# Twelve gate and value pairs by Strassen instead of eleven, in a fused attention and two-layer MoE kernel on one core

## The chip, the cores and the metric

One Trainium2 chip, one of its cores. The time is the device time of one execution in microseconds (us). TensorE (PE) multiplies matrices, VectorE (DVE) and ScalarE (ACT) work element by element, GpSimd (POOL) does a little of the same, and SyncE (SP) issues nearly all DMAs. Each engine takes its own instructions strictly in the order in which the program lists them and waits at the head of its list until the semaphores of that instruction are set.

## The reference, cut to what matters

```python
attn = softmax(causal(q @ k.T / 8)) @ v            # 2 x 12 heads, 448 tokens, 64 wide
x = attn as [896 tokens, 768]
h = x @ w_in;  g = h * clip(h + 3, 0, 6) / 6       # d_ff 2048
y = g @ w_out                                      # [896, 768]
rms = sqrt(mean(y * y, axis=-1) + 1e-6)
yn = y / rms * rms_g
out = (silu(yn @ w_gate) * (yn @ w_val)) @ w_out2  # d_ff 1536
```

The change touches the step from `y` to the products with `w_gate` and `w_val`.

## The kernel before, in words

Tokens lie on the free axis: the 896 tokens are two groups, 0 and 1, of NT = 448. The 768 features are six blocks of 128 partitions, the 1536 hidden features of the second MLP twelve blocks, each with a gate and a value block: a pair m.

Every product of two fp32 numbers is made of three matmuls in fp32r (`mm3`): each operand is split into a high half (a cast on ACT) and a low half (the difference to it, on DVE), and high x high, low x high and high x low are summed in PSUM. A matmul is always 128x128 weights by 128x448 data.

A pair is a product of 2x2 blocks: gate and value weights over two halves of the features (KH = 3 blocks each), times the activations of group 0 and group 1 over the same halves. Done plainly it takes 8 block products of 9 matmuls, 72 in all. By Strassen (the Winograd form) it takes 7, that is 63, with sums of weights (`pair_first`, `pair_second`) and sums of activations. The products are numbered 1 to 7: 1 and 2 need activations of group 0 alone; 7 needs group 0 minus group 1; 6, 5, 4 and 3 need further sums of both. In the names, `yhi7_0` and `ylo7_0` are the halves of block 0 of the activations of product 7, `pthi2_7` and `ptlo2_7` the halves of pair 2's weights for product 7, `phi0_1` and `plo0_1` pair 0's value weights (products 4 and 3), `phi0_0` its gate weights (products 1 and 2).

The program is written in steps. In one step the generator `products()` emits 9 matmuls (AFTER), and `at(d, fn)` lets `fn` emit its ACT, DVE or SP instructions d steps later. So the delays set where an instruction stands in its engine's list; the semaphores set when it runs.

Before the change the first MLP's output product for group 1, `ff1_out(1)`, ends; `ff1_y` evicts each of its six blocks from PSUM and squares it. A matmul with ones (`rms_sum`, named n1) adds the squares over the partitions, `rms_root` takes the root (ACT) and the reciprocal (DVE), and `y_scale` multiplies the six blocks of group 1 by it. Only then can products with group 1 run. In the meantime PE has work with group 0: pair 0 is done plainly (PLAIN = 1, `ff2_plain`), its four block products with group 0 first, then products 1 and 2 of pairs 1 and 2, and then pair 0's four block products with group 1, which need scaled blocks but no sums. After these come the products 7, 6, 5, 4, 3 of pairs 1 and 2, then pair after pair. `y_sums`, `y_more` and `y_last` make the sums, `y_split` and `y_low` their halves.

Weights come as 768 KB loads into four `raw` buffers, are narrowed on ACT (two instructions), joined on DVE (`pair_early_join`) and, for Strassen, summed and split. Pairs 1 and 2 are loaded early, in steps 12, 14, 18 and 20 of `ff1_out(1)` (EARLY); the plain pair comes through the ordinary weight stream (`w_load`, `w_split`, `w_join`).

Of the kernel before, what the change touches and what calls it, by code (L numbers as in the profile page):

```python
# [13 lines left out]
AF = mybir.ActivationFunctionType  # L14
# [7 lines left out]
NK = DM // 128  # L22
# [3 lines left out]
NF2 = FF2 // 128  # L26
NT = B * HS
NP1 = 16
# [1 line left out]
ORDER = (1, 5, 6, 7, 3, 4, 2)  # L30
NSLOT = 75
PREPS = (2, 3.6, 8), (1, 3, 4)
EARLY = (12, 14), (18, 20)
PLAIN = 1
LATE = 10
MASK = -8e9
NRAW, NC_BUF, NW = 4, 3, 5
# [14 lines left out]
def fused_kernel(ctx: ExitStack, tc, qa, qb, ka, kb, v, w_in, w_out, w_gate, w_val, w_out2, rms_g, out):  # L52
# [5 lines left out]
    nc = tc.nc  # L58
# [50 lines left out]
    srcs, kept, parts = [], {}, {}  # L109
    for a in (w_in, w_out):  # L110
        srcs += [a[n] for n in range(NP1)]
    for name in ("in", "out"):
        srcs += [(name, n) for n in range(NP1)]
    for m in range(PLAIN):
        srcs += [w_gate[m], w_val[m]]
    IN2 = 4 * NP1
    OUT2 = IN2 + 2 * PLAIN
    srcs += [(p, n) for p in ORDER for n in range(NN)]
    raws, plain, splits = {}, {}, {}

# [76 lines left out]
    used = set()  # L197

    def w_tile(n, j):

        if n not in used and not IN2 <= n < OUT2:
            used.add(n)
            splits.pop(n - 2, None)
            at(1, w_split)
        return tuple(t[:, j * 128:(j + 1) * 128] for t in splits[n])

    def mm3(ps, w, x, first, last, again=False):

# [239 lines left out]
    def ff1_out(g, w0):  # L448


        for m in range(NK):
            ps = psum(f"y{g}_{m}")[:, :NT]
            for k in range(NF1):
                i = m * NF1 + k
                yield from mm3(ps, w_tile(w0 + i // 6, i % 6), gs[g, k], k == 0, k == NF1 - 1)
            soon(ff1_y, g, m, ps)
        for k in range(NF1):
            gs.pop((g, k))

# [149 lines left out]
    def rms_root(g, ps):  # L609
        nc.scalar.activation(ri[g], ps, AF.Sqrt, bias=eps, scale=1.0 / DM)  # L610
        nc.vector.reciprocal(ri[g], ri[g])
        for k in range(NK):
            at(1 + (k // 2 if g else 2 * k), y_scale, g, k)
        if g:
            for j in range(KH):
                at((5, 6, 6)[j], y_sums, j)

    KH = NK // 2
    ops = {}

    def y_scale(g, k):
        y = ys[g, k]
        nc.vector.tensor_mul(y, y, ri[g])
        at(1, y_split, {(0, 0): 1, (0, 1): 2, (1, 0): 0, (1, 1): 4}[g, k // KH], k % KH, y)

    def y_split(q, j, src):
        hi = slot([128, NT], f"yhi{q}_{j}", F32R)
# [2 lines left out]
        ops[q, j] = (hi, lo)  # L630
        at(1, y_low, q, j, hi, lo, src)

    done = set()

    def y_low(q, j, hi, lo, src):
        nc.vector.tensor_sub(lo, src, f32(hi))
        done.add((q, j))

    def y_sums(j):

        assert (0, j) in done and (4, j) in done
        a21, a22 = ys[1, j], ys[1, j + KH]
        nc.vector.tensor_add(a22, a21, a22)
        nc.vector.tensor_sub(a21, ys[0, j], a21)
        at(1, y_split, 5, j, ys[1, j + KH])
        at(1, y_split, 7, j, ys.pop((1, j)))
        at(1, y_more, j)

    def y_more(j):
        a11 = ys.pop((0, j))  # L650
        nc.vector.tensor_sub(a11, ys.pop((1, j + KH)), a11)
        at(1, y_split, 6, j, a11)
        at((4, 5, 5)[j], y_last, j, a11)

    def y_last(j, s2):
        a12 = ys.pop((0, j + KH))
        nc.vector.tensor_sub(a12, a12, s2)
        at(1, y_split, 3, j, a12)


    ss, spare = {}, []

    def ff2_plain(w0):

        a, b = PLAIN, PLAIN + 1
        splits.pop(w0 - 2, None)
        splits.pop(w0 - 1)
        at(1, pair_third, b)
        at(1, pair_high, b, 0)
        at(2, pair_low, b, 0)  # L670
        for i in range(2):
            at(6 + i, pair_load, b + 1, i)
        at(9, pair_high, a, 1)
        at(13, pair_low, a, 1)
        at(11, pair_high, b, 1)
        at(14, pair_low, b, 1)
        for g in range(2):
            for i in range(2):
                ps = psum(f"f{g}_{i}")[:, :NT]
                for k in range(NK):  # L680
                    q = ((1, 2), (0, 4))[g][k // KH]
                    yield from mm3(ps, w_tile(w0 + i, k), ops[q, k % KH], k == 0, k == NK - 1)
                if i == 0:
                    at(1 if g else 3, ff2_gate, g, 0, ps)
                else:
                    at(2, ff2_val, g, 0, ps)
                if g == 0:
                    spare.append(ps)
                else:
                    splits.pop(w0 + i)  # L690
            if g == 0:
                yield from ff2_products((q, m) for q in (1, 2) for m in (a, b))
        for j in range(KH):
            ops.pop((0, j))

    def ff2_gate(g, m, ps):
        t = slot([128, NT], f"t{g}_{m}")
        nc.scalar.activation(t, ps, AF.Silu)
        ss[g, m] = t

    def ff2_val(g, m, ps):
        t = ss.pop((g, m))
        nc.vector.tensor_mul(t, ps, t)
        left_ready(g, m, t)


    praw, pc, ph = {}, {}, {}
# [7 lines left out]
    def pair_early(m, loads):  # L715

        for i in range(2):
            at(loads[i], pair_load, m, i)
            at(loads[i] + 5, pair_early_narrow, m, i)
        at(loads[1] + 7, pair_first, m)  # L720
        at(loads[1] + 8, pair_second, m)

    def pair_early_narrow(m, i):
        raw = praw.pop((m, i))
        narrowed(f32(raw[:, :, 1]), raw, False)
        at(1, pair_early_join, m, i, raw)

    def pair_early_join(m, i, raw):
        pc[m, i] = []
# [94 lines left out]
    fb, fh = {}, {}  # L824

    def ff2_strassen():
        a, b = PLAIN, PLAIN + 1
        order = [(7, a), (7, b), (6, a), (6, b), (5, a), (4, a), (5, b), (3, a), (4, b)]
        for m in range(b + 1, NF2):
            order += [(1, m), (3, m - 1)] + [(q, m) for q in (7, 6, 2, 5, 4)]  # L830
        order.append((3, NF2 - 1))
        yield from ff2_products(order)
        spare.clear()

    def ff2_products(order):
        b = PLAIN + 1
        for q, m in order:
            if (q, m) == (7, b) or q == 1 and b < m < NF2 - 1:
                pair_begin(m + 1)
            if q == 1 and m + 1 == NF2:  # L840
                state["limit"] = len(srcs)
                for n in range(NC_BUF):
                    at(1 + n, w_load)
                for n in range(NW - 1):
                    at(4 + n + 3 * (n // 3), w_split)
                for p in range(NF2 // 2):
                    at(1 + p // 2, a_fetch, ORDER[0], p)
                    at(4 + p // 2, a_split, ORDER[0], p)
                for p in range(3):
                    at(5 + p, a_fetch, ORDER[1], p)  # L850
            name = {1: "x", 2: "x", 7: "r", 4: "r"}.get(q, "y")
            if q in (1, 7):
                fb[name, m] = psum(f"f{name}_{m}")[:, :NT]
            ps = fb[name, m]
            for j in range(KH):
                yield from mm3(ps, pair_tile(q, m, j), ops[q, j], q in (1, 7) and j == 0, j == KH - 1,
                               q not in (1, 7))
                if m == NF2 - 1:
                    ops.pop((q, j))
            soon(ff2_combine, q, m)  # L860
# [58 lines left out]
    def products():  # L919
        yield from ff1_in(0, 0)  # L920
        yield from ff1_out(0, NP1)
        plan_preps(0, *PREPS[0])
        yield from ff1_in(1, 2 * NP1)
        plan_preps(PREPS[0][2], *PREPS[1])
        for m, loads in enumerate(EARLY, PLAIN):
            pair_early(m, loads)
        at(EARLY[0][1] + 9, pair_third, PLAIN)
        at(30, pair_high, PLAIN, 0)
        at(31, pair_low, PLAIN, 0)
        yield from ff1_out(1, 3 * NP1)  # L930
        yield from ff2_plain(IN2)
        yield from ff2_strassen()
        yield from strassen(OUT2)

# [116 lines left out]
```

## Time and profile before

| | |
|---|---|
| median of 3 runs | 572.06 us (571.95 to 573.84) |
| profiled execution | 571.2 us |
| its span | 569.4 us |
| PE busy | 559.0 us (98%), 3039 matmuls |
| DVE busy | 411.9 us (72%) |
| ACT busy | 391.7 us (69%) |
| granted TensorE clock, mean | 0.997 of full speed |

Busy shares are averages over the span; matmuls overlap, so PE at 98% does not say that it ran without waits. The chain of waits names what ended last at each step; the timeline gives start, duration and the idle time before an instruction, with the engine that ended it. Times in the timeline count from the start of the span.

### The profile page before, as it was taken

The numbers are of one execution on the slowest core, as the hardware profiler recorded it, in microseconds if no ns is written. First come the engines' busy times: TensorE is split into PE (matmuls) and PEld (weight loads), VectorE is DVE, ScalarE is ACT, GpSimd is POOL, SyncE is SP. The second block draws the span as 40 slices with busy tenths as digits, with TensorE's granted clock in tenths as the row PEclk, the third lists the DMA queues.
The fourth block names the chain that finished last, engine by engine and source line by source line (L and its number), as shares of the span: only waits on it lengthen the run. The fifth ranks groups of instructions, "written<-read, shape, count | busy, mean of one in ns | idle before, by whom it ended". The sixth has DMA issues, their size and how long they took to land.

```text
span 569.4 us, 9052 instructions
## 1 busy us (share of the span) xinstructions
PE 559.0 (98%) x3039; PEld 488.9 (86%) x3039; DVE 411.9 (72%) x809; ACT 391.7 (69%) x774; POOL 83.8 (15%) x130
## 2 busy tenths in 40 slices
PE   8799999999999999999999999999999999999997
PEld 6457777777899999999999998899999999999996
DVE  4776676867654645999666769988987976966861
ACT  7997878888876855887574858665767664754430
POOL 4665626262200100000000100000000000000000
PEclk9989999999999999999999999999999999999999
DMA  8958676765587964799899803063745607685841
GB/s 225 293 167 265 221 247 207 247 209 199 190 295 264 328 225 169 229 316 386 302 349 398 290 0 129 0 253 135 282 147 189 223 34 261 195 274 194 279 142 64
DMA packets 51231, 125.59 MB, mean 221 GB/s; under 512 B 6768, under 2 KB 30256, under 8 KB 51184
## 3 DMA queue, kind: packets, MB, share of 16 engines
q1 hardware_dynamic: 50752, 124.66, 64.5%
q8 instruction: 24, 0.39, 0.3%
q10 hardware_dynamic: 432, 0.34, 0.2%
q14 instruction: 23, 0.19, 0.1%
HBM read 93.36 MB, written 31.62 MB: 220 GB/s over the span
## 4 chain that ended last, share of the span: by engine, by line
PE 89%; ACT 6%; DVE 3%; issue 1%; ACTq 0%; DVEq 0%
PE y L211 8%; PE y L215 8%; PE y L213 8%; PE h L215 7%; PE h L211 7%; PE h L213 7%; ACT sm L338 4%; PE f L211 4%; PE f L213 4%; PE f L215 4%; PE o L398 3%; PE t L372 3%; PE s L321 3%; PE fr L213 2%; PE fr L215 2%; PE fr L211 2%
## 5 line engine op out<-in xcount | busy, mean ns | idle before, releaser
L193 DVE TENSOR_TENSOR wlo<-c,whi 128x768 fp32r<-128x768 f32 x87 | 85.1, 983 | 20.1 <-ACT whi L187 19.1
L187 ACT CAST whi<-c 128x768 fp32r<-128x768 f32 x87 | 72.3, 837 | 34.1 <-DVE c L171 16.0
L215 PE MATMUL h<-xh,wlo 128*128 128x448 f32 x192 | 71.4, 372 | 0.0
L213 PE MATMUL h<-xl,whi 128*128 128x448 f32 x192 | 70.8, 369 | 0.0
L211 PE MATMUL y<-ghi,whi 128*128 128x448 f32 x192 | 70.5, 367 | 0.0
L211 PE MATMUL h<-xh,whi 128*128 128x448 f32 x192 | 70.3, 366 | 0.0
L215 PE MATMUL y<-ghi,wlo 128*128 128x448 f32 x192 | 69.7, 363 | 0.0
L213 PE MATMUL y<-glo,whi 128*128 128x448 f32 x192 | 69.3, 361 | 0.0
L356 POOL TENSOR_SCALAR sm<-sm,st 112x112 f32<-112x112 f32 (+1 forms) x96 | 55.7, 598 | 70.0 <-ACT ghi L441 26.4
L338 ACT ACTIVATE sm<-sm,st 112x112 f32<-112x112 f32 (+3 forms) x96 | 49.7, 529 | 3.3 <-DVE st L331 3.3
L171 DVE SCALAR_TENSOR_TENSOR c<-c,raw 128x768 uint32<-128x768 uint32 x34 | 34.9, 1025 | 17.8 <-ACT raw L166 12.7
L215 PEld LDWEIGHTS h<-xh,wlo 128*128 128x128 f32 x192 | 36.0, 188 | 9.5 <-issue 6.8
L331 DVE CUSTOM_DVE_ANT_0 sm<-s,mask 112x112 f32<-112x112 f32 (+3 forms) x96 | 37.3, 443 | 5.8 <-PE s L321 5.5
L211 PEld LDWEIGHTS h<-xh,whi 128*128 128x128 f32 x192 | 36.0, 188 | 3.4 <-DVE st L331 0.7
L215 PEld LDWEIGHTS y<-ghi,wlo 128*128 128x128 f32 x192 | 35.9, 187 | 3.5
L213 PEld LDWEIGHTS h<-xl,whi 128*128 128x128 f32 x192 | 36.0, 188 | 2.7
L213 PEld LDWEIGHTS y<-glo,whi 128*128 128x128 f32 x192 | 36.0, 188 | 2.7
L211 PEld LDWEIGHTS y<-ghi,whi 128*128 128x128 f32 x192 | 36.0, 188 | 2.3
L602 POOL TENSOR_TENSOR sq<-sq,sq 128x448 f32<-128x448 f32 x8 | 9.3, 1159 | 168.8 <-ACT sq L591 138.2
L372 PE MATMUL t<-ident,sm 112*112 112x112 f32 x240 | 30.9, 268 | 2.4 <-POOL sm L356 2.0
L398 PE MATMUL o<-pt,v 112*64 112x224 f32 (+1 forms) x288 | 29.3, 334 | 2.5 <-DMA v<-in_v 1.6
L372 PEld LDWEIGHTS t<-ident,sm 112*112 112x112 f32 x240 | 23.4, 134 | 9.5 <-POOL sm L356 4.6
(174 smaller groups left out, 1344.2 us busy)
## 6 DMA issues: line engine op xcount, KB each, us to landing
raw<-in_w_in SPq DMA_DIRECT2D x16, 768.0 KB, 5.6
raw<-in_w_out SPq DMA_DIRECT2D x16, 768.0 KB, 4.9
braw<-in_w_out SPq DMA_DIRECT2D x12, 768.0 KB, 6.5
praw<-in_w_gate SPq DMA_DIRECT2D x11, 768.0 KB, 5.7
praw<-in_w_val SPq DMA_DIRECT2D x11, 768.0 KB, 6.3
c<-kept SPq DMA_DIRECT2D x21, 384.0 KB, 3.1
a<-left SPq DMA_DIRECT2D x35, 224.0 KB, 3.9
keptin<-c SPq DMA_DIRECT2D x16, 384.0 KB, 2.7
```

The lines of the kernel that those rows point to most:

```text
L171: nc.vector.scalar_tensor_tensor(bits, bits, 3, z, ALU.logical_shift_left, ALU.bitwise_or)
L187: nc.scalar.copy(hi, c)
L193: nc.vector.tensor_sub(lo, c, f32(hi))
L211: nc.tensor.matmul(ps, whi, xhi, start=first, stop=False, skip_group_check=again)
L213: nc.tensor.matmul(ps, whi, xlo, start=False, stop=False, skip_group_check=again)
L215: nc.tensor.matmul(ps, wlo, xhi, start=False, stop=last, skip_group_check=again)
L321: nc.tensor.matmul(ps[:C, o:o + n], tq[64 * j:64 * j + 64, i * C:(i + 1) * C], tk[64 * j:64 * j + 64, 0:n], start=True, stop=True)
L331: nc.vector.tensor_tensor_reduce(dst, src, mask[:, S - n:], scale=-0.125, scalar=3e38, op0=ALU.add, op1=ALU.min, accum_out=st[u][:, 0, c:c ...
L338: nc.scalar.activation(dst, dst, AF.Exp, scale=-1.0, bias=st[u][:, 0, c:c + 1], accum_out=st[u][:, 1, c:c + 1])
L356: nc.gpsimd.tensor_scalar(t[:, o:o + n], t[:, o:o + n], c, 1.0, op0=ALU.mult, op1=ALU.mult)
L372: nc.tensor.transpose(banks[-1][:C, o:o + C], t[:, o0 + kc * C:o0 + (kc + 1) * C], ident[:C, :C])
L398: nc.tensor.matmul(ps[64 * j:64 * j + 64, HS - n:HS], tv[:, kc, 64 * j:64 * j + 64], t[:, o:o + n], start=kc == 0, stop=kc == nk - 1)
```

## The change

All twelve pairs go through `ff2_strassen`; `ff2_plain`, its Silu and product helpers and `PLAIN` are gone. PE's list begins with products 1 and 2 of pairs 0, 1 and 2 (six products, 54 matmuls), all with group 0 alone, then 7 of pair 0, 7 of pair 1, 6 and 6, 7 of pair 2, 5 and 4 of pair 0, 6 of pair 2, and so on. Three pairs are loaded early. The sums of group 1 are written in the order in which the products need them: three blocks scaled, the three sums of product 7, the other three scaled, then the sums of 6, of 5 and 4, and of 3. The three spare PSUM tiles are now those of `ff1_out(1)`, blocks 1 to 3, so in the lists below a product's result may be named `y1_1`.

```diff
-EARLY = (12, 14), (18, 20)
-PLAIN = 1
+EARLY = (8, 10), (14, 16), (20, 22)
...
-    for m in range(PLAIN):
-        srcs += [w_gate[m], w_val[m]]
-    IN2 = 4 * NP1
-    OUT2 = IN2 + 2 * PLAIN
+    OUT2 = 4 * NP1
...
             soon(ff1_y, g, m, ps)
+            if g and 1 <= m < 4:
+                spare.append(ps)
...
         nc.vector.reciprocal(ri[g], ri[g])
-        for k in range(NK):
-            at(1 + (k // 2 if g else 2 * k), y_scale, g, k)
         if g:
             for j in range(KH):
-                at((5, 6, 6)[j], y_sums, j)
+                y_scale(1, j)
+            at(1, y_first)
+        else:
+            for k in range(NK):
+                at(1 + 2 * k, y_scale, 0, k)
...
+    def y_first():
+
+        for j in range(KH):
+            nc.vector.tensor_sub(ys[0, j], ys[0, j], ys[1, j])
+            y_split(7, j, ys[0, j])
+        for j in range(KH):
+            y_scale(1, j + KH)
+        at(1, y_second)
+
+    def y_second():
+
+        for j in range(KH):
+            t = slot([128, NT], f"y2_{j}")
+            nc.vector.tensor_sub(t, ys[1, j + KH], ys.pop((0, j)))
+            ys[2, j] = t
+            y_split(6, j, t)
+        at(3, y_third)
+
+    def y_third():
+
+        for j in range(KH):
+            t = ys.pop((1, j))
+            nc.vector.tensor_add(t, t, ys[1, j + KH])
+            y_split(5, j, t)
+            y_split(4, j, ys.pop((1, j + KH)))
+        at(2, y_last)
+
+    def y_last():
+
+        for j in range(KH):
+            t = ys.pop((0, j + KH))
+            nc.vector.tensor_sub(t, t, ys.pop((2, j)))
+            y_split(3, j, t)
...
-        at(loads[1] + 7, pair_first, m)
-        at(loads[1] + 8, pair_second, m)
+        if m < 2:
+            at(loads[1] + 7, pair_first, m)
+            at(loads[1] + 8, pair_second, m)
...
     def ff2_strassen():
-        a, b = PLAIN, PLAIN + 1
-        order = [(7, a), (7, b), (6, a), (6, b), (5, a), (4, a), (5, b), (3, a), (4, b)]
-        for m in range(b + 1, NF2):
+        a, b, c = range(3)
...
+        at(1, pair_third, b)
+        for i in range(2):
+            at(5 + i, pair_load, c + 1, i)
+        at(8, pair_first, c)
+        at(9, pair_second, c)
+        at(10, pair_third, c)
+        for m in (a, b, c):
+            at(7 + m, pair_high, m, 1)
+            at(10 + m, pair_low, m, 1)
+        order = [(q, m) for q in (1, 2) for m in (a, b, c)]
+        order += [(7, a), (7, b), (6, a), (6, b), (7, c), (5, a), (4, a), (6, c), (5, b), (3, a), (4, b), (5, c), (3, b), (4, c)]
+        for m in range(c + 1, NF2):
             order += [(1, m), (3, m - 1)] + [(q, m) for q in (7, 6, 2, 5, 4)]
...
         yield from ff1_out(1, 3 * NP1)
-        yield from ff2_plain(IN2)
         yield from ff2_strassen()
```

DVE's list from the reciprocal of group 1 on, before. The names `y1_k` are the blocks of group 1, `y0_k` those of group 0:

```order
L611 RECIPROCAL sq1_0_3468<-sq1_0_3468 128x448
L623 TENSOR_TENSOR y1_0_3466<-y1_0_3466,sq1_0_3468 128x448
L623 TENSOR_TENSOR y1_1_3551<-y1_1_3551,sq1_0_3468 128x448
L623 TENSOR_TENSOR y1_2_3665<-y1_2_3665,sq1_0_3468 128x448
L623 TENSOR_TENSOR y1_3_3764<-y1_3_3764,sq1_0_3468 128x448
L703 TENSOR_TENSOR t0_0_4012<-f0_1_3980,t0_0_4012 128x448
L623 TENSOR_TENSOR y1_4_3857<-y1_4_3857,sq1_0_3468 128x448
L623 TENSOR_TENSOR y1_5_3953<-y1_5_3953,sq1_0_3468 128x448
L636 TENSOR_TENSOR ylo0_0_4033<-y1_0_3466,yhi0_0_4032 128x448
```

The same place in DVE's list now:

```order
L610 RECIPROCAL sq1_0_3468<-sq1_0_3468 128x448
L624 TENSOR_TENSOR y1_0_3466<-y1_0_3466,sq1_0_3468 128x448
L624 TENSOR_TENSOR y1_1_3555<-y1_1_3555,sq1_0_3468 128x448
L624 TENSOR_TENSOR y1_2_3681<-y1_2_3681,sq1_0_3468 128x448
L641 TENSOR_TENSOR y0_0_2293<-y0_0_2293,y1_0_3466 128x448
L641 TENSOR_TENSOR y0_1_2373<-y0_1_2373,y1_1_3555 128x448
L641 TENSOR_TENSOR y0_2_2469<-y0_2_2469,y1_2_3681 128x448
L624 TENSOR_TENSOR y1_3_3783<-y1_3_3783,sq1_0_3468 128x448
L624 TENSOR_TENSOR y1_4_3874<-y1_4_3874,sq1_0_3468 128x448
L624 TENSOR_TENSOR y1_5_3957<-y1_5_3957,sq1_0_3468 128x448
L636 TENSOR_TENSOR ylo7_0_4026<-y0_0_2293,yhi7_0_4025 128x448
```

The first low half behind the reciprocal is now one of product 7; it stands tenth behind it. Before, `ylo7_0` stood twenty-fourth.

ACT's list around the root of group 1 (`sq1_0` from `n1`), before; `fx_m` holds products 1 and 2 of pair m:

```order
L785 CAST pthi2_6_3959<-pt2_6_3878 128x384
L768 CAST phi2_0_3962<-pe2_0_0_3808 128x384
L768 CAST phi2_0_3962<-pe2_0_384_3810 128x384
L610 ACTIVATE sq1_0_3468<-n1_3989,eps_73 128x448
L698 ACT_TABLE_LOAD
L698 ACTIVATE t0_0_4012<-f0_0_3944 128x448
```

And now:

```order
L752 CAST pthi1_6_3963<-pt1_6_3820 128x384
L842 COPY y1_1_3460<-fx_0_3948 128x448
L842 COPY y1_2_3552<-fx_1_3967 128x448
L842 COPY y1_3_3672<-fx_2_3984 128x448
L609 ACTIVATE sq1_0_3468<-n1_3994,eps_73 128x448
L851 ACT_TABLE_LOAD
L851 ACTIVATE s0_0_4020<-fx_0_3948 128x448
L631 CAST yhi7_0_4025<-y0_0_2293 128x448
```

Three copies of product 1 now stand ahead of the root; the last of them waits for the matmul behind n1.

PE's list where the first product 7 begins, before (behind 82 matmuls after n1):

```order
L213 MATMUL f1_1_4122<-ylo4_2_4075,whi65_3930 128x448
L215 MATMUL f1_1_4122<-yhi4_2_4074,wlo65_3931 128x448
L211 MATMUL fr_1_4177<-yhi7_0_4117,pthi1_7_3771 128x448
L213 MATMUL fr_1_4177<-ylo7_0_4118,pthi1_7_3771 128x448
L215 MATMUL fr_1_4177<-yhi7_0_4117,ptlo1_7_3772 128x448
```

And now (behind 28 matmuls after n1):

```order
L209 MATMUL fx_2_3984<-ylo2_2_3028,phi2_0_3921 128x448
L211 MATMUL fx_2_3984<-yhi2_2_3027,plo2_0_3922 128x448
L207 MATMUL fr_0_4071<-yhi7_0_4025,pthi0_7_3709 128x448
L209 MATMUL fr_0_4071<-ylo7_0_4026,pthi0_7_3709 128x448
L211 MATMUL fr_0_4071<-yhi7_0_4025,ptlo0_7_3710 128x448
```

Product 7 has moved up by 54 matmuls in PE's list, and n1 has kept its place, 26 matmuls behind the end of `ff1_out(1)`.

## Rows read from the trace of the kernel before

**Rows 1.** The page: busy time by engine, and granted clock in 40 slices.

```profile
PE 559.0 (98%) x3039; PEld 488.9 (86%) x3039; DVE 411.9 (72%) x809; ACT 391.7 (69%) x774; POOL 83.8 (15%) x130
...
PEclk9989999999999999999999999999999999999999
```

**Rows 2.** Timeline of PE: start, duration (us), line, operation, tiles, idle before and releaser.

```profile
332.12 0.37 PE L211 MATMUL f<-yhi,whi 128*128 128x448 f32 x1
...
337.38 0.91 PE L606 MATMUL n<-sq,ones 128*128 128x448 f32 x2
337.79 0.72 PE L215 MATMUL f<-yhi,wlo 128*128 128x448 f32 x1
338.34 0.37 PE L211 MATMUL f<-yhi,whi 128*128 128x448 f32 x1
...
354.72 0.36 PE L211 MATMUL fr<-yhi,pthi 128*128 128x448 f32 x1
355.48 0.47 PE L213 MATMUL fr<-ylo,pthi 128*128 128x448 f32 x1 [0.40 <-DVE ylo L636]
355.79 0.37 PE L215 MATMUL fr<-yhi,ptlo 128*128 128x448 f32 x1
...
358.13 0.36 PE L211 MATMUL fr<-yhi,pthi 128*128 128x448 f32 x1
```

**Rows 3.** Timeline of ACT, same columns.

```profile
338.33 0.64 ACT L610 ACTIVATE sq<-n,eps 128x448 f32<-128x448 f32 x1 [3.72 <-PE n L606]
338.99 1.28 ACT L698 ACT_TABLE_LOAD   x1
...
342.23 0.52 ACT L867 COPY f<-fx 128x448 f32<-128x448 f32 x1 [1.40 <-PE fx L215]
342.66 1.09 ACT L629 CAST yhi<-y 128x448 fp32r<-128x448 f32 x2
...
345.27 1.03 ACT L629 CAST yhi<-y 128x448 fp32r<-128x448 f32 x2
...
348.08 0.92 ACT L768 CAST phi<-pe 128x384 fp32r<-128x384 f32 x2
```

**Rows 4.** Timeline of DVE, same columns.

```profile
339.00 2.95 DVE L611 RECIPROCAL sq<-sq 128x448 f32<-128x448 f32 x1 [2.54 <-ACT sq L610]
341.99 2.23 DVE L623 TENSOR_TENSOR y<-y,sq 128x448 f32<-128x448 f32 x4
...
348.00 0.62 DVE L643 TENSOR_TENSOR y<-y,y 128x448 f32<-128x448 f32 x1
348.66 0.62 DVE L644 TENSOR_TENSOR y<-y,y 128x448 f32<-128x448 f32 x1
...
354.27 3.83 DVE L636 TENSOR_TENSOR ylo<-y,yhi 128x448 fp32r<-128x448 f32 x7
358.02 1.02 DVE L773 TENSOR_TENSOR plo<-pe,phi 128x384 fp32r<-128x384 f32 x2
358.95 1.16 DVE L636 TENSOR_TENSOR ylo<-y,yhi 128x448 fp32r<-128x448 f32 x2
...
368.78 1.15 DVE L636 TENSOR_TENSOR ylo<-y,yhi 128x448 fp32r<-128x448 f32 x2
```

**Rows 5.** Waits between 283 and 330 us: engine, line, releaser, total us, times, longest.

```profile
ACT y L589 <- PE y L215: 17.8, 5, 5.2
```

**Rows 6.** DMA issues between 283 and 345 us: KB each, median us to landing.

```profile
praw<-in_w_gate SPq DMA_DIRECT2D x3, 768.0 KB, 8.2
```

**Rows 7.** Stretches: busy us of PE, PEld, DVE, ACT, POOL; PE clock; DMA share; GB/s.

```profile
24.00:26.00 2.00, 0.60 (x9) 0.32 (x5) 1.97 (x8) 2.00 (x9) 1.16 (x2) 1.00 1.10 219
28.00:30.00 2.00, 2.00 (x13) 1.18 (x13) 1.97 (x8) 2.00 (x8) 1.60 (x4) 0.50 0.64 167
30.00:32.00 2.00, 2.00 (x15) 1.24 (x17) 1.01 (x8) 2.00 (x8) 1.94 (x6) 0.67 0.30 85
```

**Rows 8.** Timeline of PE in the attention stage, columns as in rows 2.

```profile
25.84 0.83 PE L372 MATMUL t<-ident,sm 112*112 112x112 f32 x3 [1.40 <-POOL sm L356]
```

More of the change, by code (lines that the diff above doesn't have):

```diff
@@ L199, in w_tile @@
     def w_tile(n, j):
-        if n not in used and not IN2 <= n < OUT2:
+        if n not in used:
             used.add(n)
@@ L417, in fused_kernel @@
     gs, ys, ri = {}, {}, {}
+    spare = []
     def ff1_in(g, w0):
@@ L623, in y_scale @@
         nc.vector.tensor_mul(y, y, ri[g])
-        at(1, y_split, {(0, 0): 1, (0, 1): 2, (1, 0): 0, (1, 1): 4}[g, k // KH], k % KH, y)
+        if g == 0:
+            at(1, y_split, 1 + k // KH, k % KH, y)
     def y_split(q, j, src):
@@ L631, in y_split @@
         at(1, y_low, q, j, hi, lo, src)
-    done = set()
     def y_low(q, j, hi, lo, src):
         nc.vector.tensor_sub(lo, src, f32(hi))
[L637 to L663, printed above, removed]
-        a, b = PLAIN, PLAIN + 1
[L666 to L692, printed above, removed]
-        for j in range(KH):
-            ops.pop((0, j))
@@ L696, in ff2_gate @@
[L696 to L704, printed above, removed]
+    def y_first():
+        for j in range(KH):
+            nc.vector.tensor_sub(ys[0, j], ys[0, j], ys[1, j])
[3 more added lines that the diff above has]
+        at(1, y_second)
@@ L725, in pair_early_narrow @@
         narrowed(f32(raw[:, :, 1]), raw, False)
-        at(1, pair_early_join, m, i, raw)
+        at(7 if (m, i) == (2, 1) else 1, pair_early_join, m, i, raw)
     def pair_early_join(m, i, raw):
@@ L826, in ff2_strassen @@
     def ff2_strassen():
-        a, b = PLAIN, PLAIN + 1
-        order = [(7, a), (7, b), (6, a), (6, b), (5, a), (4, a), (5, b), (3, a), (4, b)]
-        for m in range(b + 1, NF2):
+        a, b, c = range(3)
+        splits.pop(OUT2 - 2, None)
+        splits.pop(OUT2 - 1)
+        at(1, pair_third, b)
[10 more added lines that the diff above has]
+        for m in range(c + 1, NF2):
             order += [(1, m), (3, m - 1)] + [(q, m) for q in (7, 6, 2, 5, 4)]
         order.append((3, NF2 - 1))
[L832 to L836, printed above, removed]
         for q, m in order:
-            if (q, m) == (7, b) or q == 1 and b < m < NF2 - 1:
-                pair_begin(m + 1)
+            if (q, m) == (5, a) or q == 1 and c < m < NF2 - 1:
+                pair_begin(m + 3 if m == a else m + 1)
             if q == 1 and m + 1 == NF2:
@@ L860, in ff2_products @@
             soon(ff2_combine, q, m)
+        spare.clear()
     def ff2_combine(q, m):
@@ L924, in products @@
         plan_preps(PREPS[0][2], *PREPS[1])
-        for m, loads in enumerate(EARLY, PLAIN):
+        for m, loads in enumerate(EARLY):
             pair_early(m, loads)
-        at(EARLY[0][1] + 9, pair_third, PLAIN)
-        at(30, pair_high, PLAIN, 0)
-        at(31, pair_low, PLAIN, 0)
+            at(26 + 2 * m, pair_high, m, 0)
+            at(27 + 2 * m, pair_low, m, 0)
+        at(29, pair_third, 0)
         yield from ff1_out(1, 3 * NP1)
-        yield from ff2_plain(IN2)
         yield from ff2_strassen()
```

## The prediction, as put on record before the result was known

> **What bounds the kernel now.** I read the page first. PE is busy for 98% of the span at full clock nearly throughout [rows 1], so the time is PE's list plus PE's waits. The timeline of PE then shows where it waits around the change. `ff1_out(1)` ends and pair 0's plain products begin at 332.12; n1 starts at 337.38, 26 matmuls later; the next block begins at 338.34 and the first product 7 at 354.72 [rows 2]. Between the last two lie 81 matmuls, so one costs 16.38/81 = 0.2022 us from start to start. The first nine matmuls of product 7 take 358.13 - 354.72 = 3.41 us where 9 x 0.2022 = 1.82 would do: 1.59 us are lost to three low halves that DVE had not finished; the first shows 0.40 us as PE's idle time [rows 2]. So the chain from n1 through root, reciprocal, scaling, sums and halves was hidden but for 1.59 us behind 82 matmuls.
>
> The timelines of ACT and DVE give the prices in that chain. The root starts 0.04 us after n1's end (337.38 + 0.91) and takes 0.64; the reciprocal starts 0.03 later and the next DVE instruction 2.99 after it [rows 3, 4]. DVE starts a 128x448 instruction every 0.535 us (seven in 3.83, of which the last 0.62 is one alone), two 128x384 ones in 0.93 (358.02 to 358.95), and an instruction that reads the result of the one just before it starts 0.66 after it instead of 0.535, 0.12 more [rows 4]. From DVE's end to PE's start are 0.06 us: `ylo7_0` is the second of those seven, ends at 354.27 + 0.535 + 0.62 = 355.42, and PE goes on at 355.48 [rows 2, 4]. On ACT a PSUM copy holds the queue 0.43 (342.23 to 342.66) and is done after 0.52, a 128x448 cast holds it 0.48, a 128x384 one 0.41 [rows 3].
>
> **The change part by part.**
>
> *Fewer matmuls.* Pair 0 needs 63 instead of 72: 9 x 0.2022 = 1.82 us less on PE, which is the bound.
>
> *The old wait goes*: 1.59 us less. What is late next is the same chain, since only 28 matmuls now stand between n1 and product 7, instead of 82.
>
> *The root starts later.* The third copy of product 1 stands ahead of it on ACT and waits for the matmul that starts at 337.79 and ends at 338.51 [rows 2]. Copy at 338.56, root at 338.99, done 339.63, reciprocal at 339.66: 0.66 later than before. The table load waits for pair 0's product 2 to end (its last matmul starts at 338.34 + 8 x 0.2022 and takes 0.36: 340.3) and takes 1.28 [rows 2, 3]; with the Silu behind it ACT is free about 342, before product 7's first cast.
>
> *First new wait, product 7 of pair 0.* PE is there at 338.34 + 27 x 0.2022 = 343.80. DVE: reciprocal 339.66, then three scalings, three sums, three scalings from 342.65 on, nine at 0.535, so `ylo7_0` starts at 347.47, ends at 348.09, and PE may go on at 348.15. The high half was there by 345.5, so only the first matmul runs ahead; the third starts 0.31 after the second, as at 355.79 [rows 2], at 348.46 instead of 344.20. Lost: 4.26 us. The other two blocks come every 0.535 us and PE wants one every 0.61, so they are no wait. Product 7 of pair 1 follows, product 6 of pair 0 begins at 351.70. `ylo6_0` is six instructions behind `ylo7_0`, starts at 350.68 and is there at 351.36: in time.
>
> *Second, product 7 of pair 2.* Its weight differences were moved behind the reciprocal. DVE makes them from 352.28 (four 128x384 with two dependences, to 354.38), then three sums to 355.99, then `ptlo2_7`, done at 356.54. PE begins that product at 355.34 and needs `ptlo2_7` in its third matmul at 355.74; it gets it at 356.60. With the 0.1 for restarting: lost 0.96.
>
> *Third, product 5 of pair 0* adds into the bank from which ACT must first copy product 6. PE is there at 358.12. The copy stands on ACT behind the last cast of product 6 (350.84), a Silu, eight 128x384 casts, two copies of product 7 and six casts for products 5 and 4: it starts at about 358.70 and PE goes on at 359.28. Lost 1.16. `ylo5_0` to `ylo5_2` are there at 358.06, 359.13 and 360.20, each before its matmul.
>
> *Fourth, product 6 of pair 2* needs `ptlo2_6` in its third matmul, at 363.32. On DVE it stands behind `plo0_1`, six low halves, `plo1_1`, three sums and `ptlo2_5`; it starts at 363.59 and PE goes on at 364.20. Lost 0.98.
>
> *Cross-check.* DVE runs without a pause from 339.66: up to the first addition of pair 0's results, which product 3 of pair 0 waits for, the reciprocal, 46 further instructions and that addition come to 27.6 us by the same prices, so product 3 can't begin before 367.27. By the four waits it begins at 367.54, against 343.80 + 81 x 0.2022 = 360.18 without waits: 7.36 lost, the sum of the four. Behind it PE has waits no more: what it needs next was there a microsecond or more before. Before, the first product 3 stood 145 matmuls behind n1, now 109; it began near 358.13 + 54 x 0.2022 = 369.05, and DVE's last two low halves for it, 368.78 to 369.93 [rows 2, 4], just met it.
>
> *Edits at nothing.* The third pair's early load, narrowing and joining take the place of the plain pair's load, narrowing, joining and splitting. ACT waited 17.8 us in five waits for PE's blocks to evict in this stretch [rows 5], which covers the few instructions that come earlier; without that cover they'd cost their 0.4 to 0.9 us each. The loads start four steps (7.3 us) earlier and end with the same step; one lands in 8.2 us [rows 6], five steps (9.1 us) are given. Only a landing later by several us would stop ACT's list, and with it weight halves that PE needs. I take 0; bounds 0 and +1. From pair 3 on the order is as before.
>
> *Sum.* -1.82 - 1.59 + 4.26 + 0.96 + 1.16 + 0.98 = +3.95 us. The profiled execution took 571.2 (span 569.4), so 575.15; it was 0.86 below the median of the runs, so on the median 572.06 + 3.95 = 576.0. Bounds of what no row shows: if the root isn't held up by the copy, 0.66 less; if the three later waits don't come, 3.10 less, which leaves +0.85. I take the full sum, since DVE's total alone demands nearly all of it. Above: the clock, below.
>
> *The clock.* The new wait leaves PE nearly idle from 344.2 to 348.15 but for one matmul. In the attention stage PE idled 1.40 us before 25.84 [rows 8], in a stretch with 0.60 us busy of 2.00, and 28 to 30 us shows a granted clock of 0.50, half of 2.4 GHz, 30 to 32 a mean of 0.67: 2 x (0.5 + 0.33) / 0.5 = 3.3 us at the low level [rows 7]. At half clock 3.3 us hold some 8 matmuls fewer, 1.65 us. Put on products 7 and 6 that is mostly swallowed, since PE meets DVE and ACT again at the second to fourth wait (3.10 us in all); behind the fourth it would cost the full 1.65. The Trainium skill, page "TensorE: Matmul & The Clock Gate", section "Why this matters for your kernels", says that an idle gap between bursts of matmuls sends the array back to half rate. By that rule the dip comes here and the sum is up to 1.65 more, 577.7; the trace agrees that a gap can do it [rows 7, 8]. In the forecast I count 0 for it.
>
> **The rivals.**
>
> 1. *The clock dip costs in full*: it comes late or twice and falls where PE is the bound. For: the rows at 25.84 to 32. Against: the wait of 1.59 us at 354.72 left the clock full [rows 1, 2], and PE works densely for 7 us behind the first wait. Time 576.0 + 1.65 = 577.7.
>
> 2. *Only the first wait comes*: DVE and ACT get through the sums faster than the rows say, or PE's lost 4.26 us let them catch up. For: each of the three later waits is about 1 us. Against: they are counted with the first wait in. Time 572.06 + 0.85 = 572.9, no change that can be measured.
>
> 3. *Faster: the chain hides.* The mechanism is group 0's work as cover: if n1's result reached `ylo7_0` within the 5.5 us that 27 matmuls take, the first wait would vanish, DVE would be 4.3 us ahead, and with it the others. Time 572.06 - 3.41 = 568.65. For: the sums now stand in the order of need, the low half of product 7 tenth behind the reciprocal instead of twenty-fourth. Against: root, reciprocal and nine instructions are 0.64 + 2.99 + 4.82 + 0.62, 9.1 us, and none of the rows is noisy enough to halve that.
>
> 4. *The early loads come too late*: a landing of over 9 us holds ACT and then PE before 332. For: the DMA engines are full there. Against: ACT's five waits for PE leave it 17.8 us to catch up [rows 5]. Time 576.0 + 1 or more, 577 to 579.
>
> **How the numbers follow.** Forecast 576.0 with 0.62; the clock 0.17; only the first wait 0.13; faster 0.04; late loads 0.04. About 0.5%, 2.9 us, is what a measurement can tell from no change: below 569.2 is faster, above 574.9 slower. The forecast, the clock and late loads are slower: 0.83; only the first wait is same: 0.13; faster 0.04. The forecast's own range is 575.0 to 577.0. For 8 in 10 I take in the clock with the spread of the runs (573.84 is 1.8 above their median) and half the way to the second rival: 573.8 to 578.6.
>
> **What would show it.** PE in the changed trace: no wait up to 343.8; then the longest wait of the stage at product 7's second matmul for `ylo7_0`, ending near 348.15; waits of 0.9 to 1.2 us at product 7 of pair 2 (DVE), product 5 of pair 0 (ACT's copy) and product 6 of pair 2 (DVE); product 3 of pair 0 near 367.5; no waits from pair 3 on. DVE without a pause from 339.7 to about 368. 9 matmuls fewer. Wrong would be: product 7 beginning before 346, or a time under 574.9; the clock shows in the granted clock between 344 and 360.

## The result, and the profile after

The changed kernel takes 576.07 us (median of 4 runs, 575.60 to 576.26) against 572.00 of the kernel before on the same chip: 1.0070 times as long, 95% interval 1.0056 to 1.0085. The forecast was 576.0 us, the range 573.8 to 578.6. The profiled execution took 575.6 us (span 573.8) against 571.2 (569.4).

The page: busy time by engine, and the granted clock in 40 slices.

```profile
PE 559.0 (97%) x3030; PEld 488.4 (85%) x3030; DVE 415.4 (72%) x819; ACT 393.3 (69%) x779; POOL 84.4 (15%) x130
...
PEclk9999999999999999999999998999999999999999
```

Nine matmuls fewer than in [rows 1], and yet the same busy time: in one of the 40 slices some matmuls ran at half clock, and those last longer. The timeline of PE (start, duration in us, line, operation, tiles, idle before and releaser):

```profile
337.73 0.91 PE L605 MATMUL n<-sq,ones 128*128 128x448 f32 x2
...
345.86 0.47 PE L207 MATMUL fr<-yhi,pthi 128*128 128x448 f32 x1 [1.55 <-ACT yhi L631]
348.47 0.47 PE L209 MATMUL fr<-ylo,pthi 128*128 128x448 f32 x1 [2.14 <-DVE ylo L636]
...
349.60 0.51 PE L207 MATMUL fr<-yhi,pthi 128*128 128x448 f32 x1
...
350.28 0.57 PE L211 MATMUL fr<-yhi,ptlo 128*128 128x448 f32 x1
350.66 0.57 PE L207 MATMUL fr<-yhi,pthi 128*128 128x448 f32 x1
...
353.19 0.37 PE L209 MATMUL fr<-ylo,pthi 128*128 128x448 f32 x1
...
357.24 0.37 PE L207 MATMUL fr<-yhi,pthi 128*128 128x448 f32 x1
...
359.58 0.48 PE L207 MATMUL y<-yhi,pthi 128*128 128x448 f32 x1 [0.35 <-ACT c L848]
...
364.66 0.47 PE L211 MATMUL y<-yhi,ptlo 128*128 128x448 f32 x1 [0.75 <-DVE ptlo L757]
...
368.01 0.36 PE L207 MATMUL y<-yhi,phi 128*128 128x448 f32 x1
```

The answer to [rows 2]: n1 starts 0.35 us later than before. That offset is as large at the same sum for group 0, long before the changed part, here in the kernel before and then in the changed one:

```profile
220.15 0.91 PE L606 MATMUL n<-sq,ones 128*128 128x448 f32 x2
```

```profile
220.50 0.91 PE L605 MATMUL n<-sq,ones 128*128 128x448 f32 x2
```

So the change doesn't make it (117.23 us lie between the two sums in both), and I compare distances from n1. The first wait stands where it was forecast, in two pieces (1.55 for the cast, 2.14 for `ylo7_0`). Product 7 of pair 2 begins at 357.24 without any wait. Product 5 of pair 0 (359.58) and product 6 of pair 2 (364.66) wait, and the first product 3 begins 30.28 us behind n1. From n1 to the end of the span are 573.8 - 337.73 = 236.07 us, before 569.4 - 337.38 = 232.02: 4.05 more, 3.95 forecast.

The stretches behind the first wait (busy us of PE, PEld, DVE, ACT, POOL; PE clock; DMA share; GB/s):

```profile
348.00:350.00 2.00, 1.53 (x7) 1.40 (x8) 2.00 (x5) 0.00 (x0) 0.00 (x0) 0.92 0.00 0
350.00:352.00 2.00, 2.00 (x7) 1.79 (x6) 2.00 (x5) 1.94 (x4) 0.00 (x0) 0.50 0.03 8
352.00:354.00 2.00, 2.00 (x8) 1.81 (x8) 1.90 (x5) 2.00 (x6) 0.00 (x0) 0.73 0.00 0
```

The granted clock falls to 0.50, that is 1.2 of 2.4 GHz, behind the waits of 1.55 and 2.14 us with one matmul between them, for 2 x (0.08 + 0.50 + 0.27) / 0.5 = 3.4 us. Matmuls start every 0.375 us there (350.28, 350.66) instead of every 0.202, and the ten steps from 349.60 to 353.19 take 3.59 us instead of 2.02: 1.57 us. The Trainium skill, page "TensorE: Matmul & The Clock Gate", section "Why this matters for your kernels", has an idle gap between bursts send the array back to half rate, and this trace agrees: 0.50 behind these two waits.

The timelines of DVE and then ACT in the same stretch, answering to [rows 4] and [rows 3]:

```profile
339.99 2.95 DVE L610 RECIPROCAL sq<-sq 128x448 f32<-128x448 f32 x1 [3.18 <-ACT sq L609]
342.98 1.70 DVE L624 TENSOR_TENSOR y<-y,sq 128x448 f32<-128x448 f32 x3
...
347.80 1.69 DVE L636 TENSOR_TENSOR ylo<-y,yhi 128x448 fp32r<-128x448 f32 x3
...
352.62 1.02 DVE L746 TENSOR_TENSOR pt<-pe,pe 128x384 f32<-128x384 f32 x2
...
367.06 0.62 DVE L854 TENSOR_TENSOR c<-y,c 128x448 f32<-128x448 f32 x1
```

```profile
338.89 0.52 ACT L842 COPY y<-fx 128x448 f32<-128x448 f32 x1 [2.06 <-PE fx L211]
339.31 0.64 ACT L609 ACTIVATE sq<-n,eps 128x448 f32<-128x448 f32 x1
...
358.99 0.54 ACT L848 COPY c<-y 128x448 f32<-128x448 f32 x1
```

DVE works without a pause from the reciprocal to the first addition at 367.06, which ends at 367.68; product 3 follows at 368.01, directly behind product 6 and without a wait of its own. The root starts 0.67 us behind n1's end, since the third copy of product 1 stands ahead of it.

### The profile page after: what moved, and what is told of

Same layout as the page of the kernel before. It is cut to its first block, busy times and chain, and to the rows that moved or that the text cites. A ratio compares the mean times of both kernels' runs of the same rounds, so it can differ in the third digit from the quotient of the medians.

```text
span 573.8 us, 9058 instructions
## 1 busy us (share of the span) xinstructions
PE 559.0 (97%) x3030; PEld 488.4 (85%) x3030; DVE 415.4 (72%) x819; ACT 393.3 (69%) x779; POOL 84.4 (15%) x130
## 4 chain that ended last, share of the span: by engine, by line
PE 89%; ACT 5%; DVE 4%; issue 1%; DMA 1%; POOL 0%; SPq 0%; DVEq 0%
PE y L207 12%; PE y L211 12%; PE y L209 11%; PE h L211 7%; PE h L207 7%; PE h L209 7%; PE o L394 3%; PE s L317 3%; PE t L368 3%; ACT sm L334 3%; PE fx L207 2%; PE fx L211 2%; PE fx L209 2%; PE fr L211 2%; PE fr L209 2%; PE fr L207 2%
## 5 line engine op out<-in xcount | busy, mean ns | idle before, releaser
L189 DVE TENSOR_TENSOR wlo<-c,whi 128x768 fp32r<-128x768 f32 x85 | 83.3, 983 | 18.2 <-ACT whi L183 17.4
L183 ACT CAST whi<-c 128x768 fp32r<-128x768 f32 x85 | 70.8, 837 | 34.2 <-DVE c L167 15.6
L167 DVE SCALAR_TENSOR_TENSOR c<-c,raw 128x768 uint32<-128x768 uint32 x32 | 33.0, 1031 | 17.0 <-ACT raw L162 11.8
L394 PEld LDWEIGHTS o<-pt,v 112*64 112x64 f32 x288 | 19.2, 136 | 14.3 <-ACT pt L378 2.8
```

What stands on the lines that cost most here:

```text
L167: nc.vector.scalar_tensor_tensor(bits, bits, 3, z, ALU.logical_shift_left, ALU.bitwise_or)
L183: nc.scalar.copy(hi, c)
L189: nc.vector.tensor_sub(lo, c, f32(hi))
L394: nc.tensor.matmul(ps[64 * j:64 * j + 64, HS - n:HS], tv[:, kc, 64 * j:64 * j + 64], t[:, o:o + n], start=kc == 0, stop=kc == nk - 1)
```

## The experiments

All are edits of the changed kernel. "n1 to product 3" is the start of the first product 3 less the start of n1 in the profiled execution; without waits and at full clock it would be 22.80 us by the prediction's own count (360.18 - 337.38). From the first product 3 to the end of the span lie 205.8 us in the changed kernel and in every experiment (205.75 to 205.85), so that what an edit brings is seen between n1 and product 3.

| kernel | median us | ratio to before, 95% interval | n1 to product 3 | PE's waits in between, us |
|---|---|---|---|---|
| changed | 576.07 | 1.0070 (1.0056 to 1.0085) | 30.28 | 1.55, 2.14, 0.35, 0.75; half clock |
| e1 | 576.08 | 1.0065 (1.0050 to 1.0081) | 30.28 | 1.55, 0.54, 0.53, 1.21, 0.85, 0.74 |
| e2 | 575.20 | 1.0056 (1.0038 to 1.0074) | 29.63 | 0.91, 2.14, 0.36, 0.77; half clock |
| e3 | 576.11 | 1.0069 (1.0052 to 1.0085) | 30.27 | 0.31, 0.79, 0.86, 0.74 |
| e4 | 574.80 | 1.0043 (1.0026 to 1.0060) | 29.86 | 1.55, 2.15; half clock |
| e7 | 574.27 | 1.0042 (1.0028 to 1.0055) | 28.43 | 0.31, 1.09 |
| e8 | 573.38 | 1.0026 (1.0016 to 1.0037) | 27.77 | 0.91, 0.54, 0.53, 1.53 |
| e9 | 572.54 | 1.0017 (0.9998 to 1.0035) | 26.66 | 0.54, 0.54, 1.54 |
| e10 | 575.40 | 1.0066 (1.0053 to 1.0079) | 29.39 | 0.91, 0.54, 0.53, 1.52, 1.44 |
| e12 | 571.46 | 0.9990 (0.9975 to 1.0005) | 25.97 | 0.91, 0.54, 0.53 |
| e11 | 570.36 | 0.9972 (0.9957 to 0.9988) | 24.89 | 0.54, 0.54 |

The theory: DVE's list behind the reciprocal, by its start and its length, sets when product 3 begins, and the four waits are only where PE feels it. Strictly it is the list up to `ptlo2_6`, for which PE waits last: from there PE has 16 matmuls of its own up to product 3, 3.35 us (364.66 to 368.01), and DVE's addition is done 0.33 us before product 3 starts. The main rival: the first wait, the long one, is the price.

**e1: product 7's low halves further ahead.**

```diff
 def y_first():
-        for j in range(KH):
-            y_scale(1, j + KH)
         at(1, y_second)
 def y_second():
+        for j in range(KH):
+            y_scale(1, j + KH)
```

> Product 7's three low halves stand 7th to 9th behind the reciprocal on DVE, in front of the second three scalings, instead of 10th to 12th: 3 x 0.535 us = 1.6 us earlier. The list behind the reciprocal keeps its length. Theory (the length of DVE's list up to product 3 sets the time): the wait for ylo7 at PE falls from 2.1 us to about 0.5 us, what is gained there comes back at product 6 or at the waits for ptlo2_7 and ptlo2_6, the first product 3 starts at 368.0 +- 0.3 us as in the changed kernel, time 576.1 +- 0.3 us. Rival (the first wait is the price, and whatever shortens it pays): first product 3 at 366.4 us, time 574.5 us.

PE's timeline in e1:

```profile
338.00 0.91 PE L605 MATMUL n<-sq,ones 128*128 128x448 f32 x2
...
347.13 0.47 PE L209 MATMUL fr<-ylo,pthi 128*128 128x448 f32 x1 [0.54 <-DVE ylo L636]
...
351.95 0.47 PE L209 MATMUL y<-ylo,pthi 128*128 128x448 f32 x1 [0.53 <-DVE ylo L636]
...
357.30 0.47 PE L211 MATMUL fr<-yhi,ptlo 128*128 128x448 f32 x1 [1.21 <-DVE ptlo L757]
...
359.84 0.47 PE L207 MATMUL y<-yhi,pthi 128*128 128x448 f32 x1 [0.85 <-ACT c L848]
...
364.94 0.47 PE L211 MATMUL y<-yhi,ptlo 128*128 128x448 f32 x1 [0.74 <-DVE ptlo L757]
...
368.28 0.37 PE L207 MATMUL y<-yhi,phi 128*128 128x448 f32 x1
```

The first wait lost its 1.60 us, the clock stayed full, and product 3 still begins 30.28 us behind n1, to the hundredth. The gain comes back as a wait at product 6, a wait for `ptlo2_7` of 1.21 us that the changed kernel did not show, and a longer third wait (0.85 instead of 0.35). The rival's 574.5 us is out.

**e2: root ahead of the third copy on ACT.**

```diff
-            soon(ff2_combine, q, m)
+            (at if (q, m) == (1, c) else lambda d, *e: soon(*e))(1, ff2_combine, q, m)
```

> The square root stands ahead of the third copy of product 1 on ACT, so the reciprocal and all of DVE's list behind it begin 0.66 us earlier (the copy's time by its row). Theory (the list's start plus its length sets the time): both waits at product 7 end 0.66 us earlier, first product 3 at 367.35 us, time 575.4 us. Rival (the waits swallow one another, or the delayed copy makes PE wait at pair 2's product 2): time 576.1 us, no change, with a wait for the copy in PE's list.

29.63 us from n1 to product 3, 0.65 less than in the changed kernel where 0.66 was expected; the time fell by 0.87 us, to 575.20. Moving the start of the list moves the end by as much.

**e3: matmuls in the gap.**

```diff
+            if (q, m) == (2, c):
+                fill = psum("fill")[:, :NT]
+                for _ in range(18):
+                    nc.tensor.matmul(fill, ph[a, "t", 7][0][:, :128], ops[2, 0][0], start=True, stop=True)
```

> Eighteen more matmuls, whose sum nothing reads, stand on PE between pair 2's product 2 and pair 0's product 7: 18 x 0.202 = 3.64 us, less than the 4.26 us that PE waits there, so they push nothing back by themselves. PE then is without work for some 0.5 us instead of 4 us ahead of product 7. Theory (the half clock from 349.6 to 352.9 us followed from the wait, and it was swallowed by the later waits, since DVE's list set product 3 in any case): granted clock 1.00 throughout, the waits for ptlo2_7 (about 1 us), for the copy of product 6 (about 1.2 us) and for ptlo2_6 (about 1 us) come back to what was predicted without the dip, first product 3 at 368.0 us, time 576.1 +- 0.3 us. Rival (the half clock costs its 1.65 us in full): first product 3 at 366.4 us, time 574.4 us.

PE's timeline in e3:

```profile
338.27 0.91 PE L605 MATMUL n<-sq,ones 128*128 128x448 f32 x2
...
344.68 3.81 PE L838 MATMUL fill<-yhi,pthi 128*128 128x448 f32 x18
...
349.01 0.47 PE L209 MATMUL fr<-ylo,pthi 128*128 128x448 f32 x1 [0.31 <-DVE ylo L636]
...
357.56 0.47 PE L211 MATMUL fr<-yhi,ptlo 128*128 128x448 f32 x1 [0.79 <-DVE ptlo L757]
...
368.54 0.36 PE L207 MATMUL y<-yhi,phi 128*128 128x448 f32 x1
```

Full clock, the forecast's second wait is there (0.79), and product 3 stands at 30.27 us. So the half clock of the changed kernel had cost nothing that the later waits would not have cost, and the gap has room for 18 matmuls, 3.6 us of work, at no price.

**e4: pair 2's differences ahead of the reciprocal.**

```diff
-        if m < 2:
-            at(loads[1] + 7, pair_first, m)
-            at(loads[1] + 8, pair_second, m)
+        at(loads[1] + 7, pair_first, m)
+        at(loads[1] + 8, pair_second, m)
...
-        at(8, pair_first, c)
-        at(9, pair_second, c)
-        at(10, pair_third, c)
+        at(2, pair_third, c)
```

> Pair 2's four differences and the low halves of them stand ahead of the reciprocal on DVE, where DVE is idle for 3.2 us in the changed kernel. Behind the reciprocal seven instructions of 384 columns are gone, 7 x 0.465 = 3.3 us. Theory (the list's length sets product 3): the first waits at product 7 stay (4.3 us in all) or grow by what the seven exceed the idle time, the waits for ptlo2_7 and ptlo2_6 are gone, first product 3 between 364.8 us (the half clock swallowed) and 366.4 us (half clock in full), time 572.9 to 574.5 us. Rival (the first wait alone is the price, or PE is held by the copies on ACT): first product 3 at 368 us, time 576 us.

Both waits for pair 2's low halves are gone, and yet the median is 574.80 us, just above the expected range. The stretches behind the first wait in e4, columns as above:

```profile
348.00:350.00 2.00, 0.92 (x3) 0.83 (x4) 2.00 (x4) 0.00 (x0) 0.00 (x0) 0.60 0.01 4
350.00:352.00 2.00, 2.00 (x7) 1.78 (x6) 2.00 (x5) 1.31 (x3) 0.00 (x0) 0.50 0.03 8
352.00:354.00 2.00, 2.00 (x7) 1.78 (x6) 2.00 (x5) 2.00 (x6) 0.00 (x0) 0.50 0.00 0
354.00:356.00 2.00, 2.00 (x8) 1.79 (x8) 1.85 (x4) 1.13 (x3) 0.00 (x0) 0.69 0.00 0
```

The half clock lasted longer here than in the changed kernel, and no later wait swallowed it. It and the waits are all that is left: 29.86 - 22.80 - 4.23 for the waits at product 7, which are those of the changed kernel, makes 2.8 us of half clock. The six executions of e4 lie between 573.91 and 575.78 us, this profile being the slowest; those of the changed kernel lie within 0.66 us.

**e7: e4 and e3 in one.**

> e4_diffs_early and e3_fill in one: pair 2's seven narrow sums stand ahead of the reciprocal, and eighteen matmuls whose sum nothing reads (3.64 us) stand in PE's wait ahead of product 7. Theory (with DVE's list 3.3 us shorter nothing later swallows the half clock, so in e4 it cost what it took, and without it the gain of the shorter list is whole): granted clock 1.00 from 332 us on, no wait for a narrow low half, first product 3 some 3 us nearer to the second half's sum on PE than in the changed kernel, time 572.9 to 573.3 us. Rival (the half clock cost nothing in e4; something else holds product 3 there): as e4, 574.8 us.

PE's timeline in e7:

```profile
337.64 0.91 PE L605 MATMUL n<-sq,ones 128*128 128x448 f32 x2
...
358.66 0.47 PE L207 MATMUL y<-yhi,pthi 128*128 128x448 f32 x1 [1.09 <-ACT c L849]
...
366.07 0.37 PE L207 MATMUL y<-yhi,phi 128*128 128x448 f32 x1
```

The clock is full and product 3 comes 1.43 us earlier than in the profile of e4, so in that profile the half clock did cost. That it costs as much in e4's time is not shown: the profile was e4's slowest execution, and the two ratios to the kernel before, 1.0043 and 1.0042, can't be told apart. Against the changed kernel 3 us were expected, and 1.85 came between n1 and product 3 (1.80 in the median, 574.27 us): behind DVE's list the next bound is ACT's. The copy of product 6, for which product 5 waits 1.09 us, stands behind six casts of plain high halves, two copies and six casts of operands. I had this wait in the prediction, and left it out of this expectation.

**e8: e1, e2 and e4 in one.**

> e1, e2 and e4 in one: the list on DVE begins 0.66 us earlier, is 3.3 us shorter, and product 7's low halves stand 1.6 us further ahead in it. Theory: with the list no longer the bound, moving the low halves ahead now pays, which it did not in e1: waits at product 7 fall to 0.9 and 0.5 us, one of about 0.5 us at product 6, first product 3 between 3.9 and 5.2 us nearer to the second half's sum than in the changed kernel, time 570.9 to 572.2 us, clock full throughout. Rival (order within the list never matters, only its length and start): 0.66 us below e4, 574.1 us. Second rival (the half clock comes all the same and costs in full): 572.5 to 573.8 us.

573.38 us, above the expected 570.9 to 572.2: the three short waits are as expected and the clock is full, but the copy of product 6 holds PE for 1.53 us, a wait that none of the three theories had. Against e7, which has the full clock too, product 3 is 0.66 us earlier, and that is the root's share alone. So the first rival had the mechanism right, if not the time: moving the low halves ahead kept the clock full without a fill, and brought nothing beyond that.

**e9: e8, with a logarithm and an exponential on ACT instead of root and reciprocal.**

```diff
-        nc.scalar.activation(ri[g], ps, AF.Sqrt, bias=eps, scale=1.0 / DM)
-        nc.vector.reciprocal(ri[g], ri[g])
+        nc.scalar.activation(ri[g], ps, AF.Ln, bias=eps, scale=1.0 / DM)
+        nc.scalar.activation(ri[g], ri[g], AF.Exp, scale=-0.5)
```

> e8, and the root and the 2.95 us reciprocal on DVE replaced by a logarithm and an exponential of minus half of it on ACT, each with a table load of 1.28 us ahead of it (the first where ACT is idle). The six scalings on DVE wait for 1.28 + 0.65 us instead of 2.95 us: 1.0 us earlier. Theory (the chain root, reciprocal, scalings, sums, copy, low halves sets product 7): the waits at product 7 are all but gone (0.9 and 0.5 us less 1.0 us), time 0.5 to 1.0 us below e8. Rival (the tables ACT loads hold up its copies, which PE or DVE wait for): as e8 or up to 1.3 us above it, with a wait on ACT in DVE's list.

1.11 us less than e8 from n1 to product 3, 0.84 in the median, as expected. It comes from the start of DVE's list: the first scaling begins 3.51 us behind n1's start instead of 4.61. The wait for the copy of product 6 stays at 1.54, since the whole chain moved with the list.

**e10: e8, with nine low halves on GpSimd.**

```diff
-            nc.vector.tensor_sub(l, c, f32(h))
+            (nc.gpsimd if i and m < 3 else nc.vector).tensor_sub(l, c, f32(h))
...
-        nc.vector.tensor_sub(lo, src, f32(hi))
+        (nc.gpsimd if q == 4 else nc.vector).tensor_sub(lo, src, f32(hi))
```

> e8, and nine low halves (the six of the plain value tiles and the three of product 4's operand) formed on GpSimd, which is idle there, instead of on DVE: 6 x 0.465 + 3 x 0.535 = 4.4 us less in DVE's list, at about 1.16 us each on GpSimd. Theory (in e8 what is left of PE's waits is the chain to product 7, not the list's length): time as e8, +- 0.3 us. Rival (the list still sets product 3 in e8): up to 1.3 us below e8. Second rival (GpSimd's slower low halves come late): a wait of PE for a low half of product 4, 0.5 to 2 us above e8.

2.0 us slower than e8, by a cause that no theory had. The groups by line between 352 and 368 us (count, busy us, mean ns of one, idle before), first e8, DVE; then e10, DVE; then e10, GpSimd:

```profile
L669 DVE TENSOR_TENSOR y<-y,y 128x448 f32<-128x448 f32 x3 | 1.7, 616 | 0.0
```

```profile
L669 DVE TENSOR_TENSOR y<-y,y 128x448 f32<-128x448 f32 x3 | 4.3, 1480 | 0.0
```

```profile
L739 POOL TENSOR_TENSOR plo<-pe,phi 128x384 fp32r<-128x384 f32 x6 | 9.0, 1531 | 26.1 <-ACT phi L734 26.1
```

The same three sums take 1480 ns each instead of 616 while GpSimd runs beside them. PE then waits 1.44 us at product 3 for DVE's addition.

**e11 and e12: the casts of the plain high halves further ahead on ACT, and pair 0's plain low halves on DVE**, e11 on top of e9, e12 on top of e8.

```diff
-            at(7 + m, pair_high, m, 1)
-            at(10 + m, pair_low, m, 1)
+            at((1, 6, 6)[m], pair_high, m, 1)
+            at((2, 10, 11)[m], pair_low, m, 1)
```

> e9, and ACT's six copies of the plain high halves stand further ahead: pair 0's before the second copy of product 1, pair 1's and 2's in ACT's idle 2.7 us ahead of the copies for product 6's operand, so 6 x 0.41 = 2.45 us are gone from in front of the copy of product 6, for which PE waited 1.54 us in e8 and e9; pair 0's two low halves move ahead of the scalings on DVE. Theory (with DVE's list out of the way, ACT's list up to the copy of product 6 is the next bound, 1.54 us): that wait is gone, the two of 0.54 us stay, first product 3 on PE 1.5 us nearer to the second half's sum than in e9, time 570.9 to 571.1 us, faster than the kernel before by 0.9 to 1.1 us. Rival (DVE's list up to product 3, or a wait for a low half, comes 0.5 to 1 us behind it): 571.5 to 572.0 us.

> e11 with the square root and DVE's reciprocal as in the kernel before: against e8 it moves only ACT's six copies and pair 0's two low halves. Theory: the wait of 1.53 us for the copy of product 6 is gone, those of 0.9, 0.5 and 0.5 us stay, time 571.8 to 572.0 us, the kernel before's time within 0.3 us. Rival (the next bound stands close behind): 572.5 us.

PE's timeline in e11:

```profile
337.52 0.91 PE L605 MATMUL n<-sq,ones 128*128 128x448 f32 x2
...
344.92 0.47 PE L209 MATMUL fr<-ylo,pthi 128*128 128x448 f32 x1 [0.54 <-DVE ylo L636]
...
349.74 0.47 PE L209 MATMUL y<-ylo,pthi 128*128 128x448 f32 x1 [0.54 <-DVE ylo L636]
...
362.41 0.37 PE L207 MATMUL y<-yhi,phi 128*128 128x448 f32 x1
```

The wait for the copy is gone in both, 1.77 and 1.80 us of n1 to product 3 with it. Both are a little below the expected times (570.36 and 571.46 us). e11 is faster than the kernel before, 0.9972 (0.9957 to 0.9988); e12 can't be told from it. So with shorter lists behind n1 twelve Strassen pairs can be faster than the kernel before as it stands. That the nine saved matmuls pay by themselves is not shown: the kernel before was not given these edits, and it too loses 1.59 us to the chain behind n1 [rows 2].

## Why the prediction was right, step by step

*Fewer matmuls, the old wait*: as forecast; 3030 against 3039, and nothing answers to the 1.59 us of [rows 2].

*Edits at nothing*: forecast 0, and 0 came, since the sums of squares of group 0 and group 1 stand 117.23 us apart on PE in both kernels. The fourth rival had a part of its mechanism: between 283 and 330 us ACT waited 4.0 us in three waits for the early loads, and before not at all for these. But it still waited 9.2 us for PE's blocks (17.8 before), and PE was not held up.

*The root starts later*: forecast 0.66 us, 0.65 came back in e2.

*First wait*: forecast to end at 348.15, with the offset of 0.35 at 348.50; it ended at 348.47. Counted to the third matmul (348.78 instead of 344.55), 4.23 us were lost, 4.26 forecast.

*Second wait*: forecast 0.96, none came. DVE finished `ptlo2_7` at 356.97 (forecast 356.89 with the offset), but PE came only at 357.24, held back by the half clock. e1 and e3, at full clock, show this wait with 1.21 and 0.79 us.

*Third*: forecast 1.16, some 0.6 came, for the same reason; ACT's copy began at 358.99, forecast 359.05 with the offset.

*Fourth*: forecast 0.98; 1.02 came (364.66 instead of 363.74, and 0.1 for restarting).

*The clock*: it fell behind the first wait, as the prediction had allowed for, cost 1.57 us where it fell, and took the place of the second wait and half of the third: 4.23 + 1.57 + 0.6 + 1.02 = 7.4 us lost in all, against 7.36 forecast without it. e3 shows it: without the half clock the time is the same. So the first rival, the dip in full, is out for the changed kernel.

*Sum*: from n1 to the end 4.05 us more, forecast 3.95; in the medians 4.07.

What the prediction had wrong is its form. It put four waits in a row as terms of a sum, with DVE's total as a cross-check. By e1 they are no terms: take 1.6 us from the first, and the others grow by it. By e1, e2 and e3 the cross-check is the mechanism, and it would have been the shorter sum: start of the reciprocal plus DVE's list. It put product 3 at 367.27, with the offset at 367.62; DVE's addition ended at 367.68, and PE came 0.33 us behind that. e4 and e7 bear out the length only in part: with 3.3 us off the list the waits for pair 2's low halves are gone, but the half clock (e4) and ACT's list (e7) take much of the gain. The second rival, that only the first wait comes, had its case against it in that same total. The third, that the chain hides, gave 568.65 us; e11 shows how much must go for it: a start 1.8 us earlier, a list shorter by some 4.5 us, and ACT's copies out of the way, and it is still 1.7 us above that. Between n1 and product 3 e11 stands 2.09 us above the count without waits; by the starts of its matmuls 0.90 of them are lost at product 7 and 1.19 at product 6 of pair 0.

What the prediction did not see is how close the next bound lies. With DVE's list out of the way (e7), ACT's list holds product 5, and of the 3 us expected of e7 only 1.85 came.

Left open: why the half clock lasted 3.4 us in the changed kernel and twice that in the profile of e4 behind the same wait; and with it what the half clock costs in e4's time.

## What to carry to other kernels

Before work is taken off the bounding engine, look at which other engine's chain that work was hiding; here 54 matmuls fewer stood between n1 and the first product that needs it, and nine saved could not pay for that. Where an engine runs a list without a pause up to the point that matters, price its start plus its whole length and not the waits on the way, since shortening one wait only lengthens the next. When a list is shortened, work out the next engine's list to the same point before naming the gain.

## What the runs showed of the hardware that was not expected

GpSimd is no free helper beside a busy DVE: with both on two-operand sums in SBUF, DVE's 128x448 sum went from 616 to 1480 ns, and GpSimd's own took 1531 ns for 384 columns. The Trainium skill, page "GPSIMD Engine Reference", section "1. Specifications", says that its SBUF interfaces are shared with VectorE and contended by DVE instructions with two SBUF inputs; e10 agrees.

The half clock behind a wait of 2.14 or 2.15 us lasted 3.4 us in the changed kernel and in e2, and 2 x (0.40 + 0.50 + 0.50 + 0.31) / 0.5 = 6.8 us in the profile of e4. e1, whose two waits at product 7 are 1.55 and 0.54 us, kept the full clock.
